# The last block of a routed MLP in plain fp32 on two column tiles, a 128-byte move of four weight buffers and of an early operand, and a prefix scan issued earlier

## The chip, the cores and the metric

The kernel runs on one core of a Trainium2 chip. The metric is device microseconds of one launch, from the first instruction to the end; lower is better. Before the change the median of three runs is 790.61 us (790.17 to 790.62). One more execution was taken with the hardware profiler: it took 790.55 us, and its span, from its first to its last instruction, is 788.8 us.

## The reference, cut to what matters

Attention feeds a mixture of experts in which each token goes to one expert.

```python
# attention: q, k, v are (8, 8, 576, 64); s is (8, 8, 576)
cum = np.cumsum(np.maximum(s, 0), -1)
scores = q @ k.T / 8 + np.minimum(-(cum[:, :, :, None] - cum[:, :, None, :]), 0)   # causal mask on top
x = softmax(scores) @ v                      # back to 4608 tokens of 512
# experts: w_gate (512, 8), w1 (8, 512, 1024), w2 (8, 1024, 512)
logits = x @ w_gate + modality_bias[modality_id]
e = argmax(logits, 1); gate = softmax(logits)[e]
out[token] = gate * (relu(x[token] @ w1[e]) @ w2[e])
```

## The kernel before

**Two halves.** The first 367 us are attention: 32 head pairs in turn, each some 11 us, in class `Attn`. The rest are the experts, in class `Moe`: tokens have been scattered into one list per expert, and the lists are worked off in blocks of 256 rows, 18 of them (about 22 us each), then one last block. A loop for still more quarter blocks stands behind it; with this data it makes no trip.

**Precision.** The matmuls of the experts take the type fp32r. For the precision wanted, each operand is held as two fp32r parts, high and low (`parts`: ScalarE copies the high part, L1076; VectorE subtracts it from the raw weights, L1077), and each product is three matmuls: high by high, high by low, low by high. A weight chunk is 128 partitions by 1024 values raw (4 KB a partition, one DMA of 512 KB) and `[P, 2, 1024]` split. An expert has eight chunks: W[0..3] of w1, W[4..7] of w2.

**Buffers for chunks.** Thirteen slots take the split chunks in a fixed rotation: five of `wcb`, four of `wca`, four of `wcc0` to `wcc3`. Raw chunks land in two `wraw` and four `wrbw`. In the compiled program of before these are the byte addresses in a partition that matter below: `wca` 30,752 to 63,519; `wcb` 99,360 to 140,319; `hT` at 140,512; the two `xT` at 156,896 and 165,088; `wcc0` at 196,256 and its three fellows each 8,192 further. The pool of the `wcc` is laid down from the right end, and its last member is a `gap` of 320 bytes, so its size sets where the `wcc` lie. Block 0 has an `xT` of its own (`early_rows`), inside the tile `x` of the attention half at 217,824, from byte 128 of it on: 217,952. Its weights all lie in `wca`.

**A block of 256 rows** (`block`): `hp` (L1224) takes W[0..3] as the stationary operand and streams `xT`, 256 columns at a time: 8 x 4 x 3 = 96 matmuls. ScalarE and VectorE make `hT` of it. `second` (L1198) takes `hT` as the stationary operand and streams W[4..7], 512 columns at a time: 2 x 8 x 3 = 48 matmuls. ScalarE and VectorE scale each half by the gate into `ys`, and GpSimd scatters the rows.

**The last block** (`two`, `sums2`, `split`) works 64 rows each of two experts. It transposes them on TensorE (L1265), splits them, and makes for each expert four (w1, twice) and eight (w2) steps of two matmuls of 512 columns, in which high and low rows lie side by side as 128 stationary columns: 64 matmuls (L1284). Between them the hidden rows are added up (ScalarE L1291, VectorE L1308), transposed (L1314, four at a time) and split. At the end ScalarE moves the low rows (L1291), VectorE adds, scaled by the gate (L1323), for one expert after the other, and GpSimd scatters (L1324). Its 16 raw chunks are fetched by `weights2` through the raw buffers and split into 15 slots and a spare `xT`.

**The routing group** (`group`) runs four times, once per eight head pairs: three times in the background of the next head pair, the fourth time in block 0. VectorE makes a one-hot matrix `ohb` (L789) and a row sum `gs` (L790); ScalarE adds a constant to `gs` (L793); VectorE scans the one-hot matrix (L798) and takes a reciprocal (L799); two small matmuls with `tri` (L350 or L804) use `ohb` and `ahead`, the scan's result.

**What sets the order.** Each engine has one queue in order. The framework's scheduler lays these orders out from the program's order, priorities and its own costs; `issue_after` pins an instruction behind another. A generator's `yield` puts what follows it some steps further on in the program. Loads go through SyncE's queue in order, each behind the waits for its buffer. The framework also keeps two engines from one PSUM bank at a time.

Of the kernel before, what the change touches and what calls it, by code (L numbers as in the profile page):

```python
# [17 lines left out]
P = 128  # L18
# [657 lines left out]
class Route:  # L676
# [85 lines left out]
    def group(self, bp, x, psum, mm, then=None):  # L762
# [27 lines left out]
        nc.vector.tensor_reduce(out=gs, in_=ex, axis=AX.X, op=ALU.add)  # L790
        for _ in range(2 if mm else 0):
            yield False
# [4 lines left out]
        ahead = w.tile([P, 80], BF16, name="ahead")  # L797
        nc.vector.tensor_tensor_scan(ahead, self.go.rearrange("p e t -> p (e t)"), ohx[:, :80], 0.0, ALU.mult, ALU.add)  # L798
# [205 lines left out]
class Moe:  # L1004
# [39 lines left out]
    def fetch(self, e, j):  # L1044
# [5 lines left out]
        if j < 4:  # L1050
            d = nc.sync.dma_start(raw, self.w1[bass.ds(e, 1), P * j:P * j + P, :].rearrange("o p f -> p (o f)"))
        else:
            d = nc.sync.dma_start(raw.rearrange("p (u d) -> p u d", u=2),
                                  self.w2[bass.ds(e, 1), 256 * (j - 4):256 * (j - 4) + 256, :].rearrange("o (u p) d -> p (o u) d", u=2))
# [3 lines left out]
    def parts(self, raw, d, n, j, w=None):  # L1058
        nc = self.nc
        m = (n - self.NA) % (self.NA + self.NB + self.NC)  # L1060
        if w is not None:
            pass
        elif n < self.NA or self.NB <= m < self.NB + self.NA:
            w = self.wa.tile([P, 2, 1024], F32R, name="wca", bufs=self.NA)
        elif m < self.NB:
            w = self.wb.tile([P, 2, 1024], F32R, name="wcb", bufs=self.NB)
        else:
            w = self.wc.tile([P, 2, 1024], F32R, name=f"wcc{(m - self.NB - self.NA + 2) % self.NC}")
# [29 lines left out]
    def weights2(self, es):  # L1098

        W = [], []  # L1100

        def more():
            for j in range(8):
                for q in range(2):
                    w = None
                    if (j, q) == (6, 1):
                        w = self.mp.tile([P, 2, 4, 256], F32R, name="xT").rearrange("p a k n -> p a (k n)")
# [84 lines left out]
    def second(self, W, xg, oi, hT, ahead):  # L1192
# [9 lines left out]
        for u in range(2):  # L1202
            ys = self.my.tile([P, 512], F32, name="ys", bufs=3)
            gate = xg[1][:, u, 0:1]
            with self.tc.issue_after(self.conv[ahead][u]):
# [42 lines left out]
    def split(self, X, tp, relu=False):  # L1248

        nc = self.nc  # L1250
        a = nc.scalar.activation(X.rearrange("p k (a n) -> p k a n", a=4)[:, :, 0:4:2], tp.rearrange("p k (a n) -> p k a n", a=2), AF.Relu if relu else AF.Copy)
        for q in range(2):
            t, h, lo = tp[:, :, 64 * q:64 * q + 64], X[:, :, P * q:P * q + 64].bitcast(F32), X[:, :, P * q + 64:P * q + P]
            if relu:
                i = nc.vector.scalar_tensor_tensor(lo, t, 0.0, h, ALU.max, ALU.subtract)
            else:
                i = nc.vector.tensor_tensor(lo, t, h, ALU.subtract)
        return a, i

    def x2(self, xg):  # L1260
        nc = self.nc
        X = self.mp.tile([P, 2, 4, 256], F32R, name="xT")[:, 0]
# [3 lines left out]
        self.split(X, tp)  # L1266
        return X

    def sums2(self, o, W, parts, scale=1.0, after=(), apart=False):

        nc = self.nc
        n = len(parts)
        def order(i):
            return (0, 1) if i == 0 else (1, 0)

        if apart:

            seq = [(i, c, q) for h in range(2) for q in range(2) for i in range(n // 2 * h, n // 2 * h + n // 2) for c in order(i)]
        else:
            seq = [(i, c, q) for i in range(n) for c in order(i) for q in range(2)]  # L1280
        for i, c, q in seq:
            x, k, c0 = parts[i]
            m = 64 if c else P
            self.last[0] = nc.tensor.matmul(o[q][:m], x[:, P * q:P * q + m], W[q][k][:, c, c0:c0 + 512], start=i == 0 and c == 0, stop=i == n - 1 and c == 0)  # L1284
        lo = self.wc.tile([P, 512], F32, name="ql", bufs=2)
        for q in range(2):
            with ExitStack() as behind:
                for i in after:
                    behind.enter_context(self.tc.issue_after(i.ins))
                r = slice(64 * q, 64 * q + 64)  # L1290
                self.last[3] = nc.scalar.activation(lo[r], o[q][64:], AF.Copy, scale=scale if type(scale) is float else scale[r])  # L1291
        return lo

    def two(self, W, xg, oi, X, mid):

        nc = self.nc
        H = self.mp.tile([P, 2, 8, 256], F32R, name="hT", bufs=1)[:, 0]
        turned = ()
        for g in range(2):
            o = [self.ps.tile([P, 512], F32, name=("hp", "y")[g]) for _ in range(2)]  # L1300
            lo = self.sums2(o, W, [(X[:, k], k, 512 * g) for k in range(4)], 1.0, turned[:1])
            hs = self.wc.tile([P, 512], F32, name="hs", bufs=2)
            for q in range(2):
                r = slice(64 * q, 64 * q + 64)
                with ExitStack() as behind:
                    for i in turned[1:]:
                        behind.enter_context(self.tc.issue_after(i.ins))
                    i = nc.vector.tensor_tensor(hs[r], o[q][:64], lo[r], ALU.add)  # L1308
            self.back = (self.last[3], i)
            next(self.more, 0)  # L1310
            self.back = ()
            tp = self.ps.tile([P, 4, P], F32, name="tp")
            for m in range(4):
                nc.tensor.transpose(out=tp[:, m], in_=hs[:, P * m:P * m + P], identity=self.ident)  # L1314
            turned = self.split(H[:, 4 * g:4 * g + 4], tp, True)
        mid()
        y = [self.ps.tile([P, 512], F32, name="hp") for _ in range(2)]
        gate = xg[:, 0, 32, 0, 0:1]
        lo = self.sums2(y, W, [(H[:, f], 4 + f // 2, 512 * (f % 2)) for f in range(8)], gate, apart=True)
        ys = self.my.tile([P, 512], F32, name="ys", bufs=3)  # L1320
        for q in range(2):
            r = slice(64 * q, 64 * q + 64)
            self.last[1] = nc.vector.scalar_tensor_tensor(ys[r], y[q][:64], gate[r], lo[r], ALU.mult, ALU.add)  # L1323
# [70 lines left out]
    def early_rows(self, pool, A):  # L1394
# [7 lines left out]
        xT = b[:, 32:2080].bitcast(F32R).rearrange("p (a k n) -> p a k n", a=2, k=4)  # L1402
# [183 lines left out]
```

## Time and profile before

| | |
|---|---|
| median of three runs | 790.61 us |
| the profiled execution | 790.55 us, span 788.8 us |
| PE busy | 775.5 us, 98% of the span |
| VectorE, ScalarE, GpSimd busy | 72%, 66%, 47% |
| TensorE clock granted, mean | 0.996 |
| DMA, mean | 230 GB/s |

PE is TensorE's matmuls, PEld its weight loads, DVE VectorE, ACT ScalarE, POOL GpSimd, SP SyncE. A timeline row gives the start, the busy time, engine, line, operation, what is written from what, and how many; the bracket at its end is the idle time before it and who ended it. A matmul's record is longer than its turn, since matmuls are pipelined: the time that one costs is the distance to the next one's start. A plain fp32 matmul leaves two records.

### The profile page before, as it was taken

What the parts mean: (1) busy time and instruction counts of PE and PEld (TensorE: products, weight loads), DVE (VectorE), ACT (ScalarE), POOL (GpSimd) and SP (SyncE); (2) the same over time, 40 slices, a digit from 0 to 9 for tenths busy, and PEclk for the clock granted to TensorE, in tenths of its full rate; (3) what the DMA queues carried; (4) which work ended last, traced back from release to release, by engine and by line L of the source; (5) the groups of instructions that cost most, each with busy time, mean ns of one, the idle gap of its engine ahead of it and who ended that gap; (6) DMA issues with size and microseconds to landing.
All of it is one profiled execution on the core that took longest, in us unless ns stands there. A gap on an engine that the chain in (4) does not pass through costs nothing. (4 is left out here: it accounts for less than half of the span.)

```text
span 788.8 us, 17213 instructions
## 1 busy us (share of the span) xinstructions
PE 775.5 (98%) x5764; PEld 672.2 (85%) x5764; DVE 569.4 (72%) x1445; ACT 520.3 (66%) x1164; POOL 367.0 (47%) x386
## 2 busy tenths in 40 slices
PE   7999999999999999999999999999999999999996
PEld 6788887888878888888888999989889998989884
DVE  7676567665776667767879796887777777678664
ACT  6877878778788787886565435555555555455553
POOL 8978878898789978994710101110000010000011
PEclk9999999999999999999999999999999999999999
DMA  7467566776567765758979989878788777787750
GB/s 241 128 220 235 186 196 185 216 257 209 153 185 235 221 201 150 244 178 238 325 252 305 316 250 323 265 253 258 235 267 265 253 249 242 262 258 268 254 183 31
DMA packets 88168, 181.21 MB, mean 230 GB/s; under 512 B 13785, under 2 KB 33113, under 8 KB 87950
## 3 DMA queue, kind: packets, MB, share of 16 engines
q1 hardware_dynamic: 82238, 160.03, 65.2%
q0 software_dynamic: 5840, 20.06, 6.5%
q8 instruction: 46, 0.75, 0.4%
q14 instruction: 44, 0.36, 0.1%
HBM read 143.59 MB, written 26.80 MB: 216 GB/s over the span
## 5 line engine op out<-in xcount | busy, mean ns | idle before, releaser
L1210 POOL DMA_INDIRECT out<-ys,oi x36 | 40.4, 1122 | 340.1 <-ACT ys L1209 245.6
L431 ACT ACTIVATE pe<-pe,mx 128x512 f32<-128x512 f32 (+3 forms) x256 | 142.4, 559 | 12.9 <-DVE mx L400 12.4
L400 DVE CUSTOM_DVE_ANT_0 pe<-sp,mk 128x512 f32<-128x512 f32 (+3 forms) x256 | 116.7, 481 | 44.0 <-ACT rs L548 23.1
L455 ACT COPY PT<-pt 128x512 f32<-128x512 f32 (+1 forms) x192 | 94.2, 504 | 27.1 <-PE pt L451 27.1
L451 PE MATMUL pt<-ident,pe 128*128 128x128 f32 x640 | 105.2, 277 | 0.7 <-ACT PT L455 0.5
L376 PE MATMUL sp<-KA,QH 128*128 128x256 f32 (+2 forms) x256 | 98.9, 392 | 2.6 <-POOL KA L240 2.6
L1226 ACT ACTIVATE hT<-hp 128x512 fp32r<-128x512 f32 x72 | 43.1, 599 | 83.7 <-PE hp L1224 83.6
L330 POOL TENSOR_TENSOR QL<-rawq,QH 64x576 fp32r<-64x576 f32 x62 | 87.0, 1421 | 0.3
L330 POOL TENSOR_TENSOR KA<-rawk,KA 64x576 fp32r<-64x576 f32 x62 | 86.4, 1413 | 0.1
L1224 PE MATMUL hp<-xT,wcb 128*128 128x256 f32 x648 | 85.8, 276 | 0.0
L538 PE MATMUL o<-PT,V 128*64 128x512 f32 (+1 forms) x496 | 84.5, 440 | 0.0
L398 PE MATMUL sp<-KB,QL 76*128 76x256 f32 (+2 forms) x256 | 83.9, 330 | 0.1
L451 PEld LDWEIGHTS pt<-ident,pe 128*128 128x128 f32 x640 | 76.0, 143 | 9.0 <-ACT pe L431 1.9
L1227 DVE SCALAR_TENSOR_TENSOR hT<-hp,hT 128x512 fp32r<-128x512 f32 x72 | 49.5, 688 | 43.7 <-ACT hT L1226 43.2
L1224 PEld LDWEIGHTS hp<-xT,wcb 128*128 128x128 f32 x648 | 79.7, 188 | 0.6
L1198 PE MATMUL y<-wcb,hT 128*128 128x512 f32 x336 | 79.4, 392 | 0.0
L1198 PEld LDWEIGHTS y<-wcb,hT 128*128 128x128 f32 x336 | 62.5, 188 | 13.2
L1224 PE MATMUL hp<-xT,wca 128*128 128x256 f32 x528 | 72.3, 277 | 0.0
L1224 PEld LDWEIGHTS hp<-xT,wca 128*128 128x128 f32 x528 | 66.0, 188 | 0.7 <-DVE hT L1227 0.2
L538 PEld LDWEIGHTS sp<-PT,V 128*64 128x64 f32 x620 | 38.2, 137 | 33.3 <-issue 28.0
L1224 PE MATMUL hp<-xT,wcc 128*128 128x256 f32 x456 | 63.5, 278 | 1.5 <-DVE hT L1227 1.5
L1198 PE MATMUL y<-wcc,hT 128*128 128x512 f32 x264 | 63.3, 395 | 0.0
(305 smaller groups left out, 1689.1 us busy)
## 6 DMA issues: line engine op xcount, KB each, us to landing
wrbw<-in_w SPq DMA_DIRECT2D x104, 512.0 KB
wraw<-in_w SPq DMA_DIRECT2D x56, 512.0 KB
rawq<-in_qkv SPq DMA_DIRECT2D x31, 576.0 KB
rawk<-in_qkv SPq DMA_DIRECT2D x31, 576.0 KB
V<-in_qkv SPq DMA_DIRECT2D x32, 320.0 KB
KB<-KA SPq DMA_DIRECT2D x62, 144.0 KB
xr<-lists SPq DMA_DIRECT2D x68, 128.0 KB
lists<-z SPq DMA_DIRECT2D x8, 576.0 KB
```

What stands on the lines that cost most here:

```text
L330: self.last = nc.gpsimd.tensor_tensor(o, i, h, ALU.subtract).ins
L376: self.pe.append(self.nc.tensor.matmul(sp[:, :nn], QH[:, q0:q0 + P], self.KA[u][:, ab, :nn], start=True, stop=False).ins)
L398: self.pe.append(nc.tensor.matmul(sp[:, :nn], QL[:EXT, q0:q0 + P], KB[:EXT, ab, :nn], start=False, stop=True).ins)
L400: ins = nc.vector.tensor_tensor_reduce(out=t[:, :n], in0=sp[:, :n], in1=self.mk[:, 512 - n:512], scale=-0.125, scalar=3.0e38, op0=ALU.add, ...
L431: self.act = nc.scalar.activation(t[:, :n], t[:, :n], AF.Exp, bias=m, scale=-1.0, accum_out=st["sums"][:, o:o + 1]).ins
L451: self.pe.append(nc.tensor.transpose(out=pt[:, o:o + P], in_=pe[:, P * j:P * j + P], identity=self.ident).ins)
L455: return cp(w[:, :, :, v:v + P], pt[:, :n * (1 + both)].rearrange("p (a j q) -> p a j q", a=1 + both, q=P))
L538: m = nc.tensor.matmul(t[r, q0 - b:q1 - b], V[:, ab, j, :], PT[:, ab, PTS * j + q0 if j < 4 else PTW - 64:PTS * j + q1 if j < 4 else PTW], ...
L1198: self.last[0] = nc.tensor.matmul(y[u], hT[:, a, f, P * u:P * u + P], W[4 + f // 2][:, c, 512 * (f % 2):512 * (f % 2) + 512], start=f == 0 ...
L1224: nc.tensor.matmul(hp[:, u], W[k][:, a, f:f + P], xT[:, c, k], start=k == 0 and i == 0, stop=k == 3 and i == 2)
L1226: hi = nc.scalar.activation(hs, hp, AF.Relu)
L1227: lo = nc.vector.scalar_tensor_tensor(hT[:, 1, 2 * m:2 * m + 2], hp, 0.0, hs.bitcast(F32), ALU.max, ALU.subtract)
```

## The change

Three things.

1. **The last block.** Weights of both experts are loaded raw, without a raw buffer and without a split, straight into the slots: one slot holds chunk j of both, so there are eight slots and 16 loads. Each matmul is plain fp32, with 64 stationary columns; expert 0 writes partitions 0 to 63 of a bank and expert 1 partitions 64 to 127, so that they lie in the two column tiles of the array. There are 16 steps of two matmuls. Rectifying is done in two halves of the columns, by ScalarE and VectorE, and so is the scaling at the end; the four transposes of a group go to two banks and are copied by one engine each.
2. **Addresses.** The `gap` of the pool of `wcc` grows from 320 to 448 bytes, which moves the `wcc` down by 128 bytes. The early `xT` starts at byte 0 of its tile in place of byte 128.
3. **The scan** of the routing group is issued right behind the row sum, ahead of ScalarE's step and of the four yields around it.

```diff
-        # group, behind ScalarE's step and the yields
-        ahead = w.tile([P, 80], BF16, name="ahead")
-        nc.vector.tensor_tensor_scan(ahead, self.go..., ohx[:, :80], 0.0, ALU.mult, ALU.add)
         nc.vector.tensor_reduce(out=gs, in_=ex, axis=AX.X, op=ALU.add)
+        ahead = w.tile([P, 80], BF16, name="ahead")
+        nc.vector.tensor_tensor_scan(ahead, self.go..., ohx[:, :80], 0.0, ALU.mult, ALU.add)
...
-        self.gap(self.wc, 320)
+        self.gap(self.wc, 448)
...
-        xT = b[:, 32:2080].bitcast(F32R).rearrange("p (a k n) -> p a k n", a=2, k=4)
+        xT = b[:, :2048].bitcast(F32R).rearrange("p (a k n) -> p a k n", a=2, k=4)
...
     def weights2(self, es):
             for j in range(8):
+                w = self.slot(self.n).bitcast(F32)
+                self.n += 1
                 for q in range(2):
-                    w, d = self.parts(*self.fetch(es[q], j), w)
-                    W[q].append(w)
-                    self.hold = d.ins
-                    yield
+                    self.hold = self.load(w[:, q], es[q], j).ins
+                W.append(w)
+                yield
...
     def x2(self, xg):
-        self.split(X, tp)
+        nc.scalar.copy(X, tp)
...
+    def both(self, o, X, W, parts, steps):
+        for i in steps:
+            k, c0 = parts[i]
+            for q in range(2):
+                r = slice(64 * q, 64 * q + 64)
+                with self.tc.issue_after(self.last[0].ins):
+                    self.last[0] = self.nc.tensor.matmul(o[r], X[:, i, r], W[k][:, q, c0:c0 + 512], start=i == 0, stop=i == len(parts) - 1)
+
+    def inner(self, o, H, g):
+        hs = self.wc.tile([P, 512], F32, name="hs", bufs=2)
+        nc.scalar.activation(hs[:, :256], o[:, :256], AF.Relu)
+        nc.vector.tensor_scalar(hs[:, 256:], o[:, 256:], 0.0, None, ALU.max)
+        yield
+        for u in range(2):
+            tp = self.ps.tile([P, 2, P], F32, name=("tp", "y")[u])
+            ... two transposes ...
+            (nc.vector.tensor_copy if u else nc.scalar.copy)(H[:, 4 * g + 2 * u:4 * g + 2 * u + 2], tp)
+        yield
+
     def two(self, W, xg, oi, X, mid):
+        mid()
+        for g in range(3):
+            o = self.ps.tile([P, 512], F32, name="hp")
+            src, parts = (X, [(k, 512 * g) for k in range(4)]) if g < 2 else (H, [(4 + f // 2, 512 * (f % 2)) for f in range(8)])
+            self.both(o, src, W, parts, range(0, 2))
+            if g:
+                next(turn)
+            self.both(o, src, W, parts, range(2, len(parts)))
+            if g < 2:
+                turn = self.inner(o, H, g)
+                next(turn)
...
+        self.last[3] = nc.scalar.activation(ys[:, :256], y[:, :256], AF.Copy, scale=gate)
+        self.last[1] = nc.vector.tensor_scalar(ys[:, 256:], y[:, 256:], gate, None, ALU.mult)
...
-                self.stop = self.n + 14
```

With this the fetch order of the last block has no limit of its own any more, and `second` of the block before looks for its conversion no further than the list of conversions goes.

More of the change, by code (lines that the diff above doesn't have):

```diff
@@ L790, in group @@
         nc.vector.tensor_reduce(out=gs, in_=ex, axis=AX.X, op=ALU.add)
+        ahead = w.tile([P, 80], BF16, name="ahead")
+        nc.vector.tensor_tensor_scan(ahead, self.go.rearrange("p e t -> p (e t)"), ohx[:, :80], 0.0, ALU.mult, ALU.add)
         for _ in range(2 if mm else 0):
@@ L1049, in fetch, with load, slot, parts @@
             raw = self.wr.tile([P, 1024], F32, name="wrbw", bufs=NRB)
[L1050 to L1054, printed above, removed]
+        d = self.load(raw, e, j)
         n, self.n = self.n, self.n + 1
         return raw, d, n, j
-    def parts(self, raw, d, n, j, w=None):
-        nc = self.nc
[L1060 to L1068, printed above, removed]
+    def load(self, raw, e, j):
+        if j < 4:
+            return self.nc.sync.dma_start(raw, self.w1[bass.ds(e, 1), P * j:P * j + P, :].rearrange("o p f -> p (o f)"))
+        return self.nc.sync.dma_start(raw.rearrange("p (u d) -> p u d", u=2),
+                                      self.w2[bass.ds(e, 1), 256 * (j - 4):256 * (j - 4) + 256, :].rearrange("o (u p) d -> p (o u) d", u=2))
+    def slot(self, n):
+        m = (n - self.NA) % (self.NA + self.NB + self.NC)
+        if n < self.NA or self.NB <= m < self.NB + self.NA:
+            return self.wa.tile([P, 2, 1024], F32R, name="wca", bufs=self.NA)
+        if m < self.NB:
+            return self.wb.tile([P, 2, 1024], F32R, name="wcb", bufs=self.NB)
+        return self.wc.tile([P, 2, 1024], F32R, name=f"wcc{(m - self.NB - self.NA + 2) % self.NC}")
+    def parts(self, raw, d, n, j):
+        nc = self.nc
+        w = self.slot(n)
         n += 1
@@ L1204, in second @@
             gate = xg[1][:, u, 0:1]
-            with self.tc.issue_after(self.conv[ahead][u]):
+            with self.tc.issue_after(self.conv[min(ahead, len(self.conv) - 1)][u]):
                 if u:
@@ L1246, in xq @@
         return xT
[L1248 to L1258, printed above, removed]
     def x2(self, xg):
         nc = self.nc
-        X = self.mp.tile([P, 2, 4, 256], F32R, name="xT")[:, 0]
+        X = self.mp.tile([P, 2, 4, 256], F32R, name="xT").bitcast(F32)[:, 0, :, :P]
         tp = self.ps.tile([P, 4, P], F32, name="tp")
@@ L1265, in x2 @@
             nc.tensor.transpose(out=tp[:, k], in_=self.quads(xg, k), identity=self.ident)
-        self.split(X, tp)
+        nc.scalar.copy(X, tp)
         return X
-    def sums2(self, o, W, parts, scale=1.0, after=(), apart=False):
-        nc = self.nc
[L1272 to L1292, printed above, removed]
@@ new lines, in both @@
+    def both(self, o, X, W, parts, steps):
[6 more added lines that the diff above has]
+    def inner(self, o, H, g):
+        nc = self.nc
+        hs = self.wc.tile([P, 512], F32, name="hs", bufs=2)
[4 more added lines that the diff above has]
+            tp = self.ps.tile([P, 2, P], F32, name=("tp", "y")[u])
+            for m in range(2):
+                c = P * (2 * u + m)
+                with self.tc.issue_after(self.last[0].ins):
+                    self.last[0] = nc.tensor.transpose(out=tp[:, m], in_=hs[:, c:c + P], identity=self.ident)
+            (nc.vector.tensor_copy if u else nc.scalar.copy)(H[:, 4 * g + 2 * u:4 * g + 2 * u + 2], tp)
+        yield
@@ L1294, in two @@
     def two(self, W, xg, oi, X, mid):
         nc = self.nc
[L1297 to L1315, printed above, removed]
@@ L1316, in two @@
-        mid()
-        y = [self.ps.tile([P, 512], F32, name="hp") for _ in range(2)]
-        gate = xg[:, 0, 32, 0, 0:1]
-        lo = self.sums2(y, W, [(H[:, f], 4 + f // 2, 512 * (f % 2)) for f in range(8)], gate, apart=True)
+        H = self.mp.tile([P, 2, 8, 256], F32R, name="hT", bufs=1).bitcast(F32)[:, 0, :, :P]
+        mid()
+        turn = None
+        for g in range(3):
[8 more added lines that the diff above has]
+                next(turn)
@@ L1320, in two @@
+        y, gate = o, xg[:, 0, 32, 0, 0:1]
         ys = self.my.tile([P, 512], F32, name="ys", bufs=3)
-        for q in range(2):
-            r = slice(64 * q, 64 * q + 64)
-            self.last[1] = nc.vector.scalar_tensor_tensor(ys[r], y[q][:64], gate[r], lo[r], ALU.mult, ALU.add)
+        self.last[3] = nc.scalar.activation(ys[:, :256], y[:, :256], AF.Copy, scale=gate)
+        self.last[1] = nc.vector.tensor_scalar(ys[:, 256:], y[:, 256:], gate, None, ALU.mult)
         self.last[2] = nc.gpsimd.indirect_dma_start(
```

6 lines of the change are left out of this document (1 added, 5 removed).

## The prediction

> **What bounds the kernel now.** I read the page first, then the sums by stretch for the end, then the timeline of the last block.
>
> ```profile
> PE 775.5 (98%) x5764; PEld 672.2 (85%) x5764; DVE 569.4 (72%) x1445; ACT 520.3 (66%) x1164; POOL 367.0 (47%) x386
> ...
> 767.00:783.00 16.00, 15.82 (x73) 10.84 (x71) 10.64 (x15) 8.17 (x13) 2.43 (x2) 1.00 0.13 49
> ```
>
> PE is busy 98% of the span, and in the last block 15.82 of 16 us, which is up to its last matmul (columns: length, busy time and count of PE, PEld, DVE, ACT, POOL, the clock, the DMA share, GB/s). So time is gained where PE's own work shrinks, where PE waits, and behind PE's last matmul. The sum is made against the profiled execution, 790.55 us (span 788.8 and 1.75 around it); the median is 0.06 above.
>
> **Part 1a, the matmuls of the last block.** Now:
>
> ```profile
> 766.99 1.33 PE L1284 MATMUL hp<-wcc,xT 128*128 128x512 f32 x5
> 772.77 0.62 PE L1314 MATMUL tp<-ident,hs 128*128 128x128 f32 x4
> 773.15 1.85 PE L1284 MATMUL y<-wcb,xT 128*64 128x512 f32 x7
> 781.74 1.08 PE L1284 MATMUL hp<-wcc,hT 128*64 128x512 f32 x4
> ```
>
> From 766.99 to 781.74 + 1.08 = 782.82 PE works 15.83 us on 64 matmuls and twice four transposes (each four take 773.15 − 772.77 = 0.38). The new matmul, plain fp32 in two column tiles, isn't in this block, but attention has its very shape: two matmuls, four records, with different moving data.
>
> ```profile
> 211.98 1.08 PE L538 MATMUL o<-PT,V 128*64 128x512 f32 x4
> 212.89 0.28 PE L538 MATMUL sp<-PT,V 128*64 128x64 f32 x4
> 213.00 0.82 PE L538 MATMUL o<-PT,V 128*64 128x384 f32 x4
> 213.65 0.28 PE L538 MATMUL sp<-PT,V 128*64 128x64 f32 x4
> 213.76 0.60 PE L538 MATMUL o<-PT,V 128*64 128x256 f32 x4
> 214.20 0.28 PE L538 MATMUL sp<-PT,V 128*64 128x64 f32 x4
> ...
> 214.53 0.40 PE L538 MATMUL sp<-PT,V 128*64 128x64 f32 x8
> 214.87 0.66 PE L451 MATMUL pt<-ident,pe 128*128 128x128 f32 x4
> ```
>
> A pair costs 0.65 at 384 columns (213.00 to 213.65) and 0.44 at 256 (213.76 to 214.20); 128 columns more cost 0.21, so 512 cost 0.86. The 0.91 from 211.98 holds a start after a wait. Sixteen steps: 13.76. Eight transposes: 0.77. Changing between full array and column tiles: eight 64-column records should take twice 0.11 (212.89 to 213.00), but 0.34 pass until L451, so a change costs up to 0.12. There are five (into the block, and two into and two out of the transposes): 0.6. The last pass's tail (record 1.08 against a turn of 0.91) adds 0.17. Sum 15.30, so PE ends 0.53 sooner. Bounds of a change: 0 and 0.34; of this term: a gain of 1.1 and a loss of 0.6.
>
> The Trainium skill, TensorEngine Tiling (Array Packing), Key Properties, speaks against such alternation: a change of tiling mode drains TensorE. The row at 214.87 shows something of the sort, at 0.12; five full drains of 0.17 would make the term 0.3.
>
> Waits inside: the first sums are rectified by ACT, then DVE, about 0.9 together (rows below), while PE does two steps of the next group, 1.72. If that cover were gone, each of two turns would cost 0.9. The copies behind the transposes are needed two steps later, and feed nothing sooner.
>
> **Part 1b, behind the last matmul.**
>
> ```profile
> 782.86 0.68 ACT L1291 ACTIVATE ql<-hp,xg 64x512 f32<-64x512 f32 x1 [1.14 <-PE hp L1284]
> 783.58 0.75 DVE L1323 SCALAR_TENSOR_TENSOR ys<-hp,xg,ql 64x512 f32<-64x512 f32 x1 [1.08 <-ACTq L1558]
> 784.60 0.98 POOL L1324 DMA_INDIRECT out<-ys,oi  x1 [10.93 <-DVEq L1558]
> ...
> 364.18 0.37 ACT L495 COPY oT<-o 128x256 f32<-128x256 f32 x1 [0.80 <-PE o L492]
> 364.58 0.46 DVE L499 COPY oT<-o 64x64 f32<-64x64 f32 x2 [0.95 <-ACT oT L495]
> ```
>
> Now 782.82 to 784.60 is 1.78. Both new halves read one bank, and L499, which reads the bank that L495 reads, waited for L495's end: so ACT's half comes first, then DVE's. ACT with a gate takes 0.68 for 512 columns, a plain copy of 256 0.37; I take 0.47. For DVE, 0.48, as L1323 takes 0.75 at 512. With the hand-overs of 0.04, 0.04 and 0.27: 1.30, a gain of 0.48. Bounds: side by side 0.79 (a gain of 1.0); both as long as 512 columns, nothing gained.
>
> The loads need no room on this path: six of 16 (chunks 5 to 7) wait for the first half of the block before, whose last three matmuls start at 755.08, and are 3.1 MB. At 183 GB/s, the last slice but one of the page,
>
> ```profile
> 755.08 0.51 PE L1224 MATMUL hp<-xT,wca 128*128 128x256 f32 x3
> ...
> GB/s 241 128 220 235 186 196 185 216 257 209 153 185 235 221 201 150 244 178 238 325 252 305 316 250 323 265 253 258 235 267 265 253 249 242 262 258 268 254 183 31
> ```
>
> they take 17 us from 755.5, to 772.7; chunk 5 is wanted ten steps and the transposes in, at about 777.0. The ACT and DVE time of 16 splits is freed, but PE waited for none of them. Part 1: 1.0.
>
> **Part 2, the addresses.** They change no instruction; if they matter, the groups of one shape at different slots must differ:
>
> ```profile
> L1198 PE MATMUL y<-wcb,hT 128*128 128x512 f32 x336 | 79.4, 392 | 0.0
> L1198 PE MATMUL y<-wcc,hT 128*128 128x512 f32 x264 | 63.3, 395 | 0.0
> L1198 PE MATMUL y<-wca,hT 128*128 128x512 f32 x264 | 62.2, 392 | 0.0
> ...
> 501.01 5.63 PE L1224 MATMUL hp<-xT,wca 128*128 128x256 f32 x48
> 655.12 5.81 PE L1224 MATMUL hp<-xT,wcc 128*128 128x256 f32 x48
> 367.31 8.38 PE L1224 MATMUL hp<-x,wca 128*128 128x256 f32 x69
> ```
>
> Streaming `wcc` costs 63.3 us, `wca` 62.2, for 264 each; `wcb` at that count would be 62.4. The addresses tell why: `hT` less slot, modulo 256, is 192 for `wca` (140,512 − 30,752) and `wcb`, and 64 for `wcc` (196,256). In `hp`, `xT` less slot is 192 for `wca` and `wcb`, 64 for `wcc`, and also 64 for the early `xT` (217,952) with `wca`: and those two, all slots alike, are the slow ones (5.81 against 5.63; 69 matmuls of block 0 would be 8.0 at the pace of 501.01). A shift of 128 bytes turns each 64 into 192. So `y` gains 63.3 − 62.3 = 1.0.
>
> For `hp`: block 13 (the row at 655.12) gains 0.18 a half, but its first half ends in a wait that other engines set:
>
> ```profile
> 661.64 3.09 PE L1224 MATMUL hp<-xT,wcc 128*128 128x256 f32 x24 [0.71 <-DVE hT L1227]
> ```
>
> so 0.18 counts. Block 0 gains 0.5 for 96, of which a later wait of that kind may eat some: 0.3. Blocks with mixed slots: 0.1. Sum 0.6, bounds 0 and 1.1. Part 2: 1.6.
>
> **Part 3, the scan.** A head pair without routing takes 146.83 − 136.00 = 10.83; the one before it, the first of three with a group, takes 136.00 − 124.44 = 11.56.
>
> ```profile
> 124.44 1.08 PE L538 MATMUL o<-PT,V 128*64 128x512 f32 x4
> 136.00 0.65 PE L538 MATMUL o<-PT,V 128*64 128x512 f32 x2
> 146.83 0.65 PE L538 MATMUL o<-PT,V 128*64 128x512 f32 x2
> ...
> L798 DVE TENSOR_TENSOR_SCAN ahead<-go,ohb x4: 325/784/786, 131.7 to 371.4; 128x80 bf16<-128x80 bf16 x4
> ...
> 124.82 2.80 POOL L330 TENSOR_TENSOR KA<-rawk,KA 64x576 fp32r<-64x576 f32 x2
> 126.92 0.48 DVE L789 TENSOR_TENSOR ohb<-ox,rmx 128x72 bf16<-128x72 f32 x1
> 127.44 0.46 DVE L544 COPY oT<-sp 64x64 f32<-64x64 f32 x2
> 128.26 0.42 DVE L400 CUSTOM_DVE_ANT_0 pe<-sp,mk 128x256 f32<-128x256 f32 x1 [0.36 <-PE sp L398]
> 131.61 0.67 POOL L326 TENSOR_SCALAR QH<-rawq 128x576 fp32r<-128x576 f32 x1
> 131.66 0.79 DVE L798 TENSOR_TENSOR_SCAN ahead<-go,ohb 128x80 bf16<-128x80 bf16 x1
> 132.48 0.22 DVE L400 CUSTOM_DVE_ANT_0 pe<-sp,mk 128x128 f32<-128x128 f32 x1
> 133.62 0.19 PEld L416 LDWEIGHTS sp<-KA,QH 128*128 128x128 f32 x1 [0.20 <-DVE mx L400]
> ```
>
> The scan takes 0.79 beside a POOL operation, and 0.325 once, in block 0, where none runs. Queued behind it are the reciprocal and L400, for which PE then waits (133.62). Right behind L789 it can start at 127.40; POOL's pair ends at 127.62. At 0.33 to 0.55 it ends by 127.95, and L544 and L400 there move by 0.1 to 0.5, into an idle 0.36. Taken out, it brings L400 from 132.48 to about 131.85. The excess of 0.73 has other parts (two more matmuls, four more DVE operations behind them), so I take 0.45 of it, three times: 1.35. Bounds: 2.0 if nearly all of the excess was the scan, a loss of 0.5 if the new place delays L544 and hence PE. In the fourth group only its turn with the reciprocal changes: nothing.
>
> **Sum.** 1.0 + 1.6 + 1.35 = 3.95; 790.55 − 3.95 = 786.6 us.
>
> **The rivals.**
>
> *Distances do nothing.* The slow operands all lie above 196,000 as well, so the place and not the distance may be slow, and a move of 128 bytes leaves it. For it: no row parts the two. Against it: the two groups fall exactly by distance. 790.55 − 1.0 − 1.35 = 788.2. The Trainium skill, SBUF — State Buffer, two separate sides, says that among the engines only the port pair of VectorE and GpSimd causes contention, and that PE waits for nobody; by that rule too this part is worth nothing, though the 63.3 and 62.2 above do not fit a PE that never waits.
>
> *The scan's place gives nothing,* since the scheduler lays it elsewhere or L807 and its like hold PE as long: 790.55 − 1.0 − 1.6 = 787.95. Both rivals together: 789.55, which is no change.
>
> *Slower: the loads come late.* If SyncE's wait for a slot reaches to the end of the block before (767.0) for chunks 1 to 7, 7.3 MB start then; at 325 GB/s, the page's best slice, they land at 789.6, two more steps and the tail bring PE's end to 791.5, 9.2 later than my 782.3, and the whole to 795.8. It decides from where chunk 7 lands after 780.4, when PE wants it; slower than before by over 1.6 from 785.9. Against it: the slots of chunks 1 to 4 are last read in the second half of block 16, before the first half of block 17 that the row at 755.08 ends.
>
> **How the numbers follow.** What this kernel's measurement can tell from no change is about 0.2%, 1.6 us. Forecast 0.52, distances nothing 0.17, scan nothing 0.17, both 0.08, loads late 0.06. The range: all upper bounds together (1.1 + 1.0, 1.0 + 1.1, 2.0) would be 784.35, which needs everything at once; I end at 784.7. Upwards it takes in the first two rivals and, nearly, both together: 789.5. Out lie late loads, half of "both", and a little below. The forecast alone spans 785.2 to 788.0. Faster than 788.97: most of the forecast (0.50), of the first rival (0.14) and of the second (0.16): 0.80. Same: the rest of these and "both": 0.13. Slower: 0.07.
>
> **What would show it.** Part 1: pairs at 0.86 in L538's shape in place of L1284, PE's last matmul ending about 15.3 after the block's start, ACT's half then DVE's, POOL 1.3 behind. Part 2: `y<-wcc` at the busy time of `y<-wca`, and a first half of block 13 of 5.63. Part 3: the scan between L789 and L544, L400 some 0.6 earlier, head pairs with routing at about 11.1. Wrong I'd be by PE waits for a DMA in the last block, pairs above 1 us, or `wcc` as slow as before.

## The result, and the profile after

The changed kernel takes 786.53 us (median of five runs, 785.37 to 787.1); before, in the same session, took 790.43 (790.0 to 790.62). The ratio is 0.9947, 95% interval 0.9935 to 0.9959. The profiled execution took 786.53 us too, with a span of 784.8: 4.0 less than before. The forecast was 786.6.

The page of the changed kernel, and its sums over the last block (columns as before):

```profile
PE 772.5 (98%) x5764; PEld 667.4 (85%) x5764; DVE 544.5 (69%) x1422; ACT 501.0 (64%) x1145; POOL 366.3 (47%) x386
...
763.70:779.18 15.48, 15.47 (x73) 5.17 (x72) 2.45 (x5) 1.66 (x5) 1.96 (x2) 1.00 0.10 36
```

PE still bounds it, and has no idle time in the last block. The block's timeline in the changed kernel, from the second half of the first group on:

```profile
767.22 1.89 PE L1265 MATMUL hp<-wcc,xT 128*64 128x512 f32 x8
767.47 0.38 ACT L1271 ACTIVATE hs<-hp 128x256 f32<-128x256 f32 x1 [3.62 <-PE hp L1265]
767.88 0.42 DVE L1272 TENSOR_SCALAR hs<-hp 128x256 f32<-128x256 f32 x1 [3.28 <-ACT hs L1271]
...
769.04 0.44 PE L1279 MATMUL tp<-ident,hs 128*128 128x128 f32 x2
769.31 0.38 PE L1279 MATMUL y<-ident,hs 128*128 128x128 f32 x2
769.63 1.08 PE L1265 MATMUL hp<-wcc,xT 128*64 128x512 f32 x4
770.11 0.14 PEld L1265 LDWEIGHTS hp<-wcb,xT 128*64 128x64 f32 x2 [0.29 <-issue]
...
773.80 5.37 PE L1265 MATMUL hp<-wcb,hT 128*64 128x512 f32 x24
779.22 0.47 ACT L1301 ACTIVATE ys<-hp,xg 128x256 f32<-128x256 f32 x1 [5.16 <-PE hp L1265]
779.72 0.48 DVE L1302 TENSOR_SCALAR ys<-hp,xg 128x256 f32<-128x256 f32 x1 [5.39 <-ACT ys L1301]
780.48 0.98 POOL L1303 DMA_INDIRECT out<-ys,oi  x1 [11.87 <-DVE ys L1302]
```

The last `y` matmul of the block before starts at 763.42, and its turn is 0.23. From the end of that turn (763.65) to the end of the last block's last matmul (779.17) PE works 15.52 us, where it was 15.84 by the same measure. From there to POOL's scatter it is 1.31, where it was 1.78. ACT's half and DVE's half follow each other, in the middle of the block (767.47, 767.88) and at its end: DVE's waits end with ACT.

The experts' matmuls by slot, and the two places whose busy time had been foretold from the distance, in the changed kernel (L1199 and L1225 are L1198 and L1224 of before):

```profile
L1199 PE MATMUL y<-wcb,hT 128*128 128x512 f32 x336 | 79.5, 393 | 0.0
L1199 PE MATMUL y<-wca,hT 128*128 128x512 f32 x264 | 62.3, 392 | 0.0
L1199 PE MATMUL y<-wcc,hT 128*128 128x512 f32 x264 | 62.2, 391 | 0.0
...
365.67 8.09 PE L1225 MATMUL hp<-x,wca 128*128 128x256 f32 x69
...
652.51 5.63 PE L1225 MATMUL hp<-xT,wcc 128*128 128x256 f32 x48
659.00 2.99 PE L1225 MATMUL hp<-xT,wcc 128*128 128x256 f32 x24 [0.86 <-DVE hT L1228]
```

`wcc` fell from 63.3 to 62.2, level with `wca`. Block 13's first half took 5.63 instead of 5.81, and the wait behind it grew from 0.71 to 0.86. Block 0's 69 matmuls went from 8.38 to 8.09.

The first routing pair, and the scan (the last row is of the view of one line: shortest, median and longest in ns, first and last start):

```profile
124.80 1.08 PE L538 MATMUL o<-PT,V 128*64 128x512 f32 x4
127.81 0.22 DVE L544 COPY oT<-sp 64x64 f32<-64x64 f32 x1
127.94 0.31 DVE L792 TENSOR_TENSOR_SCAN ahead<-go,ohb 128x80 bf16<-128x80 bf16 x1
132.27 0.27 DVE L400 CUSTOM_DVE_ANT_0 pe<-sp,mk 128x128 f32<-128x128 f32 x1
135.73 1.08 PE L538 MATMUL o<-PT,V 128*64 128x512 f32 x4
...
L792 DVE TENSOR_TENSOR_SCAN ahead<-go,ohb x4: 304/306/325, 127.9 to 369.8; 128x80 bf16<-128x80 bf16 x4
```

The pair takes 135.73 − 124.80 = 10.93 instead of 11.56; the scan stands between the two L544 and takes 0.31 in place of 0.79.

**Where the 4.0 went.** Three routing pairs: 3 × 0.63 = 1.9, and 0.12 in the one before the last of them (11.10 to 10.98). The experts' blocks from the first `hp` to the last `y`: 399.44 to 397.75, 1.7. Last block: 0.32 and 0.47. That is 4.5; 0.36 was lost ahead of the first L538, which starts at 26.72 instead of 26.36.

That start moves from execution to execution: over the profiles below it lies between 26.05 and 28.31, whatever the kernel. So the table also gives the stretch from the first L538 to the end of the span, which leaves it out; it is of one profile of each kernel. "Before" ran at 790.4 to 792.4 in the sessions, which were on several chips; ratios hold within one session. For the kernels from `scan_twice` on, the ratio shows 0.4 to 1.9 us more gain, or less loss, than the stretch, so kernels of different sessions compare no better than that, and the argument below rests on single groups and blocks in the traces. One of the four executions of `split_turns` took 1549.52 us and is left out of its ratio.

| kernel | ratio, 95% interval | first L538 to the end, us |
|---|---|---|
| before | 1 | 762.48 |
| changed | 0.9947 (0.9935 to 0.9959) | 758.09 |
| block_only | 0.9989 (0.9980 to 0.9998) | 761.72 |
| addr_only | 0.9975 (0.9964 to 0.9985) | 760.28 |
| scan_only | 0.9972 (0.9960 to 0.9984) | 759.88 |
| gap576 | 0.9961 (0.9946 to 0.9976) | 759.26 |
| scan_twice | 0.9930 (0.9914 to 0.9947) | 758.86 |
| scan_old | 0.9956 (0.9941 to 0.9971) | 760.84 |
| split_turns | 0.9935 (0.9915 to 0.9954) | 758.65 |
| dist1 | 1.0055 (1.0035 to 1.0075) | 767.24 |
| dist2 | 1.0049 (1.0033 to 1.0065) | 767.56 |
| hT0 | 0.9971 (0.9961 to 0.9981) | 761.98 |
| best | 0.9968 (0.9957 to 0.9978) | 761.17 |
| best2 | 0.9961 (0.9947 to 0.9974) | 760.63 |

### The profile page after: what moved, and what is told of

Its sections match the earlier page's. It is cut to its first block, busy times and chain, and to the rows that moved or that the text cites. A ratio compares the mean times of both kernels' runs of the same rounds, so it can differ in the third digit from the quotient of the medians.

```text
span 784.8 us, 17146 instructions
## 1 busy us (share of the span) xinstructions
PE 772.5 (98%) x5764; PEld 667.4 (85%) x5764; DVE 544.5 (69%) x1422; ACT 501.0 (64%) x1145; POOL 366.3 (47%) x386
## 5 line engine op out<-in xcount | busy, mean ns | idle before, releaser
L400 DVE CUSTOM_DVE_ANT_0 pe<-sp,mk 128x512 f32<-128x512 f32 (+3 forms) x256 | 116.6, 480 | 43.0 <-ACT rs L548 24.0
L451 PE MATMUL pt<-ident,pe 128*128 128x128 f32 x640 | 106.1, 278 | 0.2 <-ACT pe L431 0.2
L376 PE MATMUL sp<-KA,QH 128*128 128x256 f32 (+2 forms) x256 | 98.6, 390 | 1.3 <-POOL KA L240 1.3
L1225 PE MATMUL hp<-xT,wcb 128*128 128x256 f32 x648 | 86.0, 277 | 0.0
L398 PE MATMUL sp<-KB,QL 76*128 76x256 f32 (+2 forms) x256 | 84.1, 330 | 1.7 <-DMA QL<-ek 1.6
L538 PE MATMUL o<-PT,V 128*64 128x512 f32 (+1 forms) x496 | 84.5, 440 | 0.0
L451 PEld LDWEIGHTS pt<-ident,pe 128*128 128x128 f32 x640 | 77.4, 144 | 7.6 <-ACT pe L431 1.4
L1225 PEld LDWEIGHTS hp<-xT,wcb 128*128 128x128 f32 x648 | 79.9, 188 | 0.6
L1199 PE MATMUL y<-wcb,hT 128*128 128x512 f32 x336 | 79.5, 393 | 0.0
L1199 PEld LDWEIGHTS y<-wcb,hT 128*128 128x128 f32 x336 | 62.5, 188 | 13.2
L1225 PE MATMUL hp<-xT,wca 128*128 128x256 f32 x528 | 72.3, 277 | 0.0
L1225 PEld LDWEIGHTS hp<-xT,wca 128*128 128x128 f32 x528 | 66.0, 188 | 0.7 <-DVE hT L1228 0.2
L538 PEld LDWEIGHTS sp<-PT,V 128*64 128x64 f32 x620 | 38.2, 137 | 33.3 <-issue 28.8
L1225 PE MATMUL hp<-xT,wcc 128*128 128x256 f32 x456 | 63.0, 277 | 1.5 <-DVE hT L1228 1.5
L1199 PE MATMUL y<-wca,hT 128*128 128x512 f32 x264 | 62.3, 392 | 0.0
```

Source lines behind the costliest of these rows:

```text
L376: self.pe.append(self.nc.tensor.matmul(sp[:, :nn], QH[:, q0:q0 + P], self.KA[u][:, ab, :nn], start=True, stop=False).ins)
L398: self.pe.append(nc.tensor.matmul(sp[:, :nn], QL[:EXT, q0:q0 + P], KB[:EXT, ab, :nn], start=False, stop=True).ins)
L400: ins = nc.vector.tensor_tensor_reduce(out=t[:, :n], in0=sp[:, :n], in1=self.mk[:, 512 - n:512], scale=-0.125, scalar=3.0e38, op0=ALU.add, ...
L451: self.pe.append(nc.tensor.transpose(out=pt[:, o:o + P], in_=pe[:, P * j:P * j + P], identity=self.ident).ins)
L538: m = nc.tensor.matmul(t[r, q0 - b:q1 - b], V[:, ab, j, :], PT[:, ab, PTS * j + q0 if j < 4 else PTW - 64:PTS * j + q1 if j < 4 else PTW], ...
L1199: self.last[0] = nc.tensor.matmul(y[u], hT[:, a, f, P * u:P * u + P], W[4 + f // 2][:, c, 512 * (f % 2):512 * (f % 2) + 512], start=f == 0 ...
```

## The experiments

**One part at a time.** Three kernels carry one part each: `block_only` the last block, `addr_only` the two address edits, `scan_only` the earlier scan.

```diff
 block_only: the changed kernel, but
-        self.gap(self.wc, 448)
+        self.gap(self.wc, 320)
-        xT = b[:, :2048]...
+        xT = b[:, 32:2080]...
 and the scan back ahead of the reciprocal
 addr_only:  the kernel before, with the first four lines reversed
 scan_only:  the kernel before, with the scan behind the row sum
```

> The new last block alone; the pool gap at 320, the early xT at byte 128 and the scan at its old place. My theory (three parts that add up): only the last block and what stands behind it gain, 0.3 on PE and 0.46 behind the last matmul, so about 789.65 against 790.4; head pairs with routing stay at 11.56, y from wcc stays at 63.3 us. Rival (the new block alone does harm elsewhere, which the other two parts only repair): 790.4 or slower.

> The kernel before with the two addresses alone (gap 448, early xT at byte 0); every engine's order of instructions is that of before. Distance theory: y from wcc falls from 63.3 to 62.3 us, block 0 and block 13 get faster, 1.4 to 1.8 in all: 788.6 to 789.0. Place theory (what lies above byte 196,000 is slow, whatever the distance): 790.4, y from wcc at 63.3.

> The kernel before with the scan at its new place alone. My theory: head pairs with routing fall from 11.56 to about 10.95, 1.9 us in all: 788.5. Rival (the gain in these head pairs comes with the other two parts): 790.4, head pairs at 11.56.

By their stretches the three are worth 0.76, 2.20 and 2.60, by their ratios 0.9, 2.0 and 2.2 us. `block_only` shows the last block as in the changed kernel (15.52 of PE, then 1.32); the 0.32 and 0.46 saved there, 0.78, are what part 1 is worth, less than the 1.0 forecast. In `addr_only` the instructions of every engine stand in the order of before, and still:

```profile
L1198 PE MATMUL y<-wcc,hT 128*128 128x512 f32 x264 | 62.2, 391 | 0.0
L1224 PE MATMUL hp<-x,wca 128*128 128x256 f32 x96 | 11.4, 279 | 0.0
```

So moving bytes alone is worth 2 us here. In `scan_only` the routing pairs are 10.89, 10.89 and 10.93. The three singles add up to 5.6, the whole gave 4.4: the missing 1.2 lies mostly in blocks 2 (23.17, against 22.46 in `scan_only`) and 0 (22.56, against 22.24 in `addr_only`). What happens there is told below, with the paces.

**Distance or place.** `gap576` is the changed kernel with the pool's gap grown by another 128 bytes: the `wcc` lie lower still, but the distance is 64 again.

```diff
-        self.gap(self.wc, 448)
+        self.gap(self.wc, 576)
```

> The kernel after with the gap at 576 bytes in place of 448: the wcc lie 128 bytes lower still, where hT less slot is 64 again modulo 256; the early xT stays where the change put it. Distance theory: y from wcc goes back to 63.3 us, block 13 is slow again, 1.0 to 1.5 are lost: 787.5 to 788.0. Place theory (lower is better, or the move as such helped): 786.5, y from wcc at 62.3.

```profile
L1199 PE MATMUL y<-wcc,hT 128*128 128x512 f32 x264 | 63.3, 395 | 0.0
L1199 PE MATMUL y<-wca,hT 128*128 128x512 f32 x264 | 62.2, 392 | 0.0
```

`wcc` is as slow as before, to the tenth. It holds over all kernels in which `hT` lies as before: `y<-wcc` takes 63.3 in the four with distance 64 (before, `block_only`, `scan_only`, `gap576`) and 62.2 or 62.3 in the five with 192 (changed, `addr_only`, `scan_twice`, `scan_old`, `split_turns`). So for `y` it is the distance, and the rival of the place falls. For `hp` more is said below.

**Other distances.** `dist1` and `dist2` shift the three pools so that `hT` less slot takes the other six multiples of 32.

```diff
 dist1 (dist2 in brackets)
-        self.gap(self.wb, 416)
+        self.gap(self.wb, 512 (480))
-        self.gap(self.mp, 96)
+        self.gap(self.mp, 160 (128))
-        self.gap(self.wc, 448)
+        self.gap(self.wc, 480 (576))
```

> The changed kernel with the gaps between the tiles grown, so that hT less the slot, modulo 256, is 96 for wca, 0 for wcb and 128 for wcc (in the changed kernel 192 for all). Theory that 64 alone is a slow distance: y<-w stays at about 229 ns a matmul for all three slots, 786.5 in all. Rival that the distance has to be 192, or in a range about it: the slots that fall outside it go to 233 ns, which is 1.1 us more for wca or wcc and 1.4 for wcb, up to 790 in all with the first halves of the blocks.

> The changed kernel with other gaps: hT less the slot, modulo 256, is 32 for wca, 224 for wcb and 160 for wcc. Theory that 64 alone is slow: 229 ns a matmul for all three, 786.5. Rival that the range about 64 is slow: wca at 231 to 233 ns and wcb and wcc at 229, 787 to 788. A distance that is faster than 192 would show as a group below 229 ns.

Both theories were too small: the kernels are 9 us slower than the changed one by their stretches, 8 to 9 by the ratios. From start to start of neighbouring matmuls the traces give, by `hT` less slot (for `y`) and `xT` less slot (for `hp`) modulo 256, means in ns of those below 350 (64 and 192 from the kernel before; each class but 192 comes from one type of slot):

```
distance   0     32    64    96    128   160   192   224
y        227.8 233.7 233.0 234.2 232.4 233.6 229.5 233.2
hp       119.4 117.4 115.5 119.5 118.7 118.7 113.9 118.4
```

So it is not that 64 is bad: 192 is good for both, 0 is better for `y`, and nearly all else is slow. For `hp` the means mix two paces, as is shown below. In the groups of `dist1`, `hp` is what costs most (89.5 where the changed kernel has 86.0):

```profile
L1225 PE MATMUL hp<-xT,wcb 128*128 128x256 f32 x648 | 89.5, 282 | 0.0
L1199 PE MATMUL y<-wcb,hT 128*128 128x512 f32 x336 | 78.8, 390 | 0.0
L1199 PE MATMUL y<-wca,hT 128*128 128x512 f32 x264 | 63.4, 396 | 0.0
```

**Distance 0 for `y`, 192 for `hp`.** `wcb` at distance 0 had 227.8. `hT0` moves `hT` by 64 bytes and keeps `xT` less slot at 192 (modulo 256) with a filler between them.

```diff
-        self.gap(self.mp, 96)
+        self.gap(self.mp, 160)
 block, behind hT, once
+        self.mp.tile([P, 48], F32, name="apart", bufs=1)
```

> The changed kernel with hT moved up by 64 bytes, so that hT less the slot is 0 modulo 256 for every slot, while xT less the slot stays at 192. The run with wcb at distance 0 had its y matmuls 227.8 ns apart, against 229.5 at 192. If that is the distance, all 864 y matmuls gain 1.6 ns, 1.4 us in all: a ratio of 0.993 or a little under, against 0.9947 of the changed kernel, and y<-wca at 61.8 or less. If it was something else in that run, y<-wca stays at 62.2 and the ratio at 0.995.

```profile
L1228 PE MATMUL hp<-xT,wcb 128*128 128x256 f32 x648 | 88.5, 281 | 0.0
L1200 PE MATMUL y<-wcb,hT 128*128 128x512 f32 x336 | 78.5, 389 | 0.0
L1200 PE MATMUL y<-wca,hT 128*128 128x512 f32 x264 | 61.6, 390 | 0.0
```

`y` did what was expected and more: 227.0 ns throughout, 2 us saved over the three slots. But `hp` went to 118, although its own distance had not changed modulo 256: from 86.0 to 88.5 for `wcb` alone. By its stretch the kernel lost 3.9 us against the changed one, by the ratios 1.9. Modulo 512 that distance had changed, from 192 to 448; that was the next theory.

**Modulo 512, and a shorter tail.** `best` is `hT0` with the last group in two column halves and two banks. `best2` moves `xT` by 256 bytes more, so that its distance is 192 modulo 512 again, and gives both last evictions to ACT.

```diff
 best
+            n = 512 if g < 2 else 256
-        self.last[1] = nc.vector.tensor_scalar(ys[:, 256:], y[:, 256:], gate, None, ALU.mult)
+        y = self.ps.tile([P, 512], F32, name="y")[:, :256]
+        self.both(y, src, W, [(k, c0 + 256) for k, c0 in parts], range(8), 256)
+        self.last[1] = nc.vector.tensor_scalar(ys[:, 256:], y, gate, None, ALU.mult)
 best2, beside it
-        self.mp.tile([P, 48], F32, name="apart", bufs=1)
+        self.mp.tile([P, 112], F32, name="apart", bufs=1)
-        self.last[1] = nc.vector.tensor_scalar(ys[:, 256:], y, gate, None, ALU.mult)
+        self.last[3] = nc.scalar.activation(ys[:, 256:], y, AF.Copy, scale=gate)
```

> hT moved as in the run beside it, and the last group of the last block in two column halves: all eight steps over columns 0 to 255 into one bank, then over 256 to 511 into another, so that ACT evicts the first half while PE makes the second, and only DVE's 0.48 us stands behind the last matmul. Worked out: 0.04 + 0.48 + 0.27 = 0.79 from the last matmul to POOL's issue instead of 1.31, so 0.5 us less than the run beside it, if a pair over 256 columns takes half of one over 512, 0.43. Rival: with half the columns a pair no longer covers the loading of the next operands and takes 0.5 or more; then the 16 pairs lose what the tail gains, or more.

> As the run before it (hT less the slot 256 modulo 512, the last group in two column halves) with two changes. xT moves up by a further 256 bytes, so that xT less the slot is 192 modulo 512 again, as in the changed kernel, and not 448 as in the two runs with hT moved; and both halves of the last eviction go to ACT, so that POOL waits for one engine alone. Theory (the distance counts modulo 512): hp<-xT goes back from 118 to 113 or 114 ns a matmul while y<-w stays at 227, so y<-wca and y<-wcc are 61.6 us, y<-wcb 78.5 and hp<-xT,wcb 86.3; with a tail of 0.8 us from the last matmul to POOL's issue instead of 1.31 the ratio is 0.9915 to 0.992. Rival (it was the move of hT that made hp slow, or the distance counts modulo 256 and something else did): hp<-xT stays at 118 and the ratio at 0.996 to 0.997. For the tail: if POOL still starts 1.3 behind the last matmul, the waiting for two engines was not the cause.

The tail first. In `best`:

```profile
782.92 0.48 DVE L1308 TENSOR_SCALAR ys<-y,xg 128x256 f32<-128x256 f32 x1 [5.78 <-PE y L1268]
784.18 0.98 POOL L1309 DMA_INDIRECT out<-ys,oi  x1 [11.89 <-DVEq L1542]
```

and in `best2`:

```profile
781.73 0.47 ACT L1308 ACTIVATE ys<-y,xg 128x256 f32<-128x256 f32 x1 [2.98 <-PE y L1268]
782.48 0.98 POOL L1309 DMA_INDIRECT out<-ys,oi  x1 [11.39 <-ACTq L1542]
```

The pairs of 256 columns cost what they should: PE's work in the last block is 15.56, against 15.52. In `best` the eviction ends at 783.40 and POOL starts 0.78 later; in `best2` it ends at 782.20 and POOL starts 0.28 later, as in the changed kernel, where the last eviction is VectorE's. In `best` POOL waits for two engines, and a wait of its own stands ahead of the scatter; with one engine to wait for, it does not. From PE's end to POOL it is 1.31 in `best` and 0.80 in `best2`: the half microsecond is there, once POOL waits for one.

The distances: `y` at 227 again, `hp` at 118 again. Modulo 512 falls. But the timeline of `best2` holds something that no distance explains:

```profile
414.13 1.22 PE L1228 MATMUL hp<-xT,wcb 128*128 128x256 f32 x9
415.19 1.07 PE L1200 MATMUL y<-wcb,hT 128*128 128x512 f32 x4
416.39 0.62 PE L1228 MATMUL hp<-xT,wcc 128*128 128x256 f32 x3
416.85 1.19 PE L1228 MATMUL hp<-xT,wcb 128*128 128x256 f32 x9
418.21 1.18 PE L1228 MATMUL hp<-xT,wcb 128*128 128x256 f32 x9
...
453.90 1.22 PE L1228 MATMUL hp<-xT,wcb 128*128 128x256 f32 x9
```

The same operands, in one run (each row's record is longer than its nine turns): nine matmuls take 1.22 (118 ns from start to start), then, behind a short stop at 416.39, 1.18 (113 ns), through half of this block and the next, and from the block that starts at 453.90 on 1.22 again to the end. The changed kernel shows the reverse at the same place:

```profile
414.57 1.18 PE L1225 MATMUL hp<-xT,wcb 128*128 128x256 f32 x9
417.26 0.62 PE L1225 MATMUL hp<-xT,wcc 128*128 128x256 f32 x3 [0.60 <-DVE hT L1228]
417.72 1.22 PE L1225 MATMUL hp<-xT,wcb 128*128 128x256 f32 x9
```

So `hp` has two paces, 113 and 118 ns, and stays in one until PE stops or turns to other matmuls; a stop need not change it (the 0.86 at 659.00 in the changed kernel does not). In the changed kernel's profile, where everything lies at 192, all but a quarter of block 0 and half of block 2 runs at 113; where `y` lies at 0, nearly all run at 118. In the changed kernel `hp` went at the slow pace for half a block behind the stop in block 2, and `y` behind it at 233 ns, as in block 0 behind its slow quarter; that, and the longer wait in block 2, is most of the gain that the three singles had and the whole did not.

But it is no price of the three parts together. `split_turns` (below) has the changed kernel's addresses and, up to the last block, the same instructions in the same order on PE, ScalarE, VectorE and GpSimd, and its profile, of another session, shows:

```profile
416.30 0.62 PE L1225 MATMUL hp<-xT,wcc 128*128 128x256 f32 x3 [0.23 <-DVE hT L1228]
...
651.75 5.82 PE L1225 MATMUL hp<-xT,wcc 128*128 128x256 f32 x48
```

In block 2 the stop is 0.23 instead of 0.60, `hp` stays at 113 and the block takes 22.46 instead of 23.17. Block 13's first half takes 5.82 at distance 192, as long as it took before at 64, and block 12 takes 22.31 instead of 21.89. Over the nine kernels with the old `hT`, that half took 5.81 in all four at 64, and at 192 it took 5.63 in three and 5.82 in two (`split_turns`, `scan_old`). So addresses and order together do not fix `hp`'s pace. What sets the pace at an entry is not settled: the distances that these runs varied have a part in it and do not give it by themselves, and nothing here separates the phase of two streams from another cause.

**What was it in the scan?** `scan_twice` adds a second scan behind the routing matmuls; `scan_old` adds one at the old place, into a tile that nothing reads any more, so that VectorE has its old work and the matmuls do not wait for it.

```diff
 scan_old, ahead of the reciprocal
+        old = ex.rearrange("p t e -> p (t e)").bitcast(BF16)[:, :80]
+        nc.vector.tensor_tensor_scan(old, self.go..., ohx[:, :80], 0.0, ALU.mult, ALU.add)
 scan_twice, behind the matmuls with tri
+        nc.vector.tensor_tensor_scan(ahead, self.go..., ohx[:, :80], 0.0, ALU.mult, ALU.add)
```

> The changed kernel with the scan made a second time into the same tile, behind the routing matmuls, so that VectorE has a scan again about where it stood before, while the first one feeds the matmuls as in the changed kernel. Theory: the gain of the move came from VectorE's time at the old place, where the scan ran 0.79 us beside a POOL operation with the reciprocal and L400 queued behind it. Then the three head pairs with routing go back from 10.93 towards 11.4 to 11.56, and the time is 787.9 to 788.4. Rival: the gain came from the routing matmuls, which no longer wait for the scan. Then the head pairs stay at 10.93 to 11.0 and the time at 786.5.

> The changed kernel with a second scan of the same operands put back at the old place, ahead of the reciprocal L799, but written into the tile ex, which nothing reads any more there; the routing matmuls still take the first scan's result. So VectorE has its work at the old place again, and only that. Theory: the three routing head pairs were slow because the scan held up VectorE for 0.79 us beside the POOL operation, with L400 queued behind it; they go back from 10.93 to about 11.5, and the time rises by 1.7 to 1.9 over the changed kernel. Rival: they were slow because the routing matmuls waited for the scan; the pairs stay at 10.93 to 11.0. Both in part, as the run with the scan made again behind the matmuls has it (10.91, 11.12, 11.12): in between.

In `scan_twice` the second scan came later than the old place (133.68 in the first pair, 0.26 long; 0.67 in the second), and the pairs took 10.91, 11.12 and 11.12. In `scan_old` it stands where it was, and as long:

```profile
124.56 0.65 PE L538 MATMUL o<-PT,V 128*64 128x512 f32 x2
131.78 0.78 DVE L800 TENSOR_TENSOR_SCAN ex<-go,ohb 128x80 bf16<-128x80 bf16 x1
132.80 0.27 PE L451 MATMUL pt<-ident,pe 128*128 128x128 f32 x1
133.13 0.42 PE L376 MATMUL sp<-KA,QH 128*128 128x384 f32 x1
135.77 1.08 PE L538 MATMUL o<-PT,V 128*64 128x512 f32 x4
```

All three pairs take 11.21. So of 0.63 a pair, 0.28 comes with VectorE's time: the wait between 132.80 and 133.13, where L376 follows L451 after 0.33 instead of 0.03. The other 0.35 goes away although VectorE does the same work: it belonged to the matmul that used the scan's result, or to the order that this wait gave PE. In before, PE starts that matmul (L350 with `ahead`, 132.50) 0.43 behind the L398 of 132.07; in the changed kernel the same L398 takes 0.24 (132.47 to 132.71), and the two `tri` matmuls follow each other at once, earlier (131.69, 131.72). So 0.19 of the 0.35 shows as a wait ahead of that matmul; the rest is not traced. The rows of before:

```profile
132.07 0.39 PE L398 MATMUL sp<-KB,QL 76*128 76x512 f32 x1
132.50 0.20 PE L350 MATMUL ox<-ahead,tri 128*128 128x80 bf16 x1
```

By its stretch `scan_old` is 2.75 slower than the changed kernel, more than these 0.84 (by the ratios 0.7). Two pairs behind a routing one take 11.23 and 11.53 instead of 10.83, where L466 comes 0.41 and 0.71 late, and three blocks of the experts run at the slow pace and take 22.31 instead of 21.89. In these two pairs PE has the changed kernel's order, and no scan is near, so this isn't counted as the scan's price; why it happens is not settled.

**The price of a change of tiling.** `split_turns` takes each group's four transposes in two visits of two, one step apart (the first `yield` is the one in `inner` behind the transposes, moved into their loop).

```diff
-        yield
+            yield
-            self.both(o, src, W, parts, range(2, len(parts)))
+            self.both(o, src, W, parts, range(2, 3))
+            if g:
+                next(turn)
+            self.both(o, src, W, parts, range(3, len(parts)))
```

> The changed kernel with the four transposes of each half of the inner layer in the last block taken in two visits of two, one step apart, so that PE changes four more times between column tiles and the whole array. Theory (each visit costs about 0.30 us in changes, as the trace of the changed kernel shows around L1281's transposes): two more visits, 0.6 us more, 787.1, and the last block's PE work 16.1 instead of 15.5. Rival (the price is a fixed wait of the first transposes for the copy of their input, so that it is not paid per change): 786.5, and 15.5.

The sums over its last block:

```profile
763.28:779.36 16.08, 16.07 (x73) 4.95 (x72) 2.45 (x5) 1.66 (x5) 1.97 (x2) 1.00 0.09 35
```

16.08 against 15.48, the same matmuls: 0.60 for two more visits, 0.15 a change. The rival, a fixed wait for the copied input, would have left 15.5, and falls.

## Why the prediction was right, and where it was not

**Part 1a** (0.53 forecast, 0.32 measured). The pair was right: 0.86, so 16 are 13.7. Two sizes were not. The transposes take 0.109 each, 0.87 for eight, and not 0.77. The changes cost 0.15 and not 0.12: the first visit shows 0.10 between the last pass (from 768.51) and the transposes at 769.04, 0.15 within them to 769.63, and 0.05 in the first pass behind (769.63 to 770.11, 0.48 for 0.43). The Trainium skill, TensorEngine Tiling (Array Packing), Key Properties, has a change drain the array; the trace agrees that a change costs time, 0.15, though no row shows what PE does in it. With five full drains of 0.17 the prediction had put this term at 0.3, and 0.32 came; that is partly luck, since 0.17 was too much by 0.02 a change and the transposes were too little by 0.10.

**Part 1b** (0.48 forecast, 0.47 measured). Right in each step: 0.47, 0.48, and hand-overs as before. That the two halves of one bank go one after the other is what the framework's rule and L499's wait said. No load came late: the last six are issued from 751.31 to 754.65, from about the end of the first half of the block before on (its last three matmuls start at 751.80), which is where the prediction had them, and no wait of PE for a DMA is in the block.

```profile
751.31 3.34 SPq L1057 DMA_DIRECT2D wcb<-in_w  x6
```

**Part 2** (1.6 forecast; 1.1 in `y<-wcc`, 0.5 in `hp<-wcc` and 0.3 in block 0 make 1.9, of which the other groups lost 0.4; `addr_only` alone gave 2.0 to 2.2). The `y` term held in size and reason: 1.0 forecast, 1.1 measured, gone again in `gap576`, where the rival of the place fell. That 64 is the slow distance was too simple, though: 192 is one of two good classes. The `hp` terms came out, block 13's half to 0.01 (5.63) and block 0 nearly (8.09 for 8.0), but not for the reason given. "5.81 against 5.63" was read as the price of a distance; it is the price of a pace, which is entered and kept, and which the same operands at 192 also show (5.82 in `split_turns`). That this half fell to the fast pace in the changed kernel's profile is partly luck. The Trainium skill, SBUF — State Buffer, two separate sides, has PE wait for nobody; 113 and 118 ns for the same operands, and 62.2 and 63.3 for the same work, say that something holds it, though not what, and not that it is another engine.

**Part 3** (1.35 forecast, 2.0 measured, the upper bound). The scan's new place, its 0.31 (0.33 to 0.55 forecast) and L400's move (132.27 − 124.80 = 7.47 into the pair instead of 8.04, 0.57 for the 0.6 forecast) came as told. The step that failed is "I take 0.45 of it": the excess of a pair was put down to L400's wait, and the rest to work that stays. `scan_old` shows 0.28 for that wait, and leaves 0.35 to the matmul that used the scan and to PE's order with it, which the prediction had counted as work that stays.

**The sum.** 0.79 + 1.9 + 2.0 is 4.7, not 3.95. The spans differ by only 4.0, since 0.36 was lost in the start-up and 0.2 in block 2 (22.95 to 23.17), where the slow pace behind the wait for `hT` ate some of part 2. The forecast was right in sign for each part, and in mechanism for part 1, for the `y` of part 2 and for the scan's move; in `hp`, and in what the scan held up, it was not or only half. Its closeness is partly errors against each other.

## What to carry to other kernels

Where two groups of one instruction and one shape differ by a per cent, compare the operands' addresses before the schedule, and look at the pace from start to start over time and in more than one profile, since it can be a state and not a constant. When an operation is moved, price the instruction that uses its result as well as those queued behind it. An eviction in two halves gains more where the halves lie in two banks, so that the first runs beside the matmuls, and where the next engine has one engine to wait for: here 0.5 us more.

## What the runs showed that was not expected

- Two paces of the same matmuls, 113 and 118 ns (`hp`, 256 columns), kept through whole blocks, changed at some stops and turns between groups and not at others, and not the same in two executions with the same addresses and order; `y` went at 227.0 ns with `hT` at distance 0, at 229.4 at 192, and at 232 to 234 elsewhere. The best of `y` and the best of `hp` were had together only for a block and a half of `best2`.
- POOL's scatter starts 0.28 behind the last eviction where it waits for one engine, and 0.78 where it waits for two.
- The scan takes 0.31 between L544's copies and 0.79 beside POOL's L326.
- The changed kernel with the tail of `best2` and its own addresses was not run; from 1.31 to 0.80 it would be worth an estimated 0.5 us by these rows.
